# A top-k attention and two MLPs: folded top-k, a one-pass mask, weight splitting on ScalarE

## The chip, the cores and the metric

One core of a Trainium2 chip runs the whole program in one launch. The metric is the device time of the execution in microseconds (us); lower is better. The engines are PE (TensorE), DVE (VectorE), ACT (ScalarE), POOL (GpSimd) and SP, which issues the transfers. Each works through a queue of its own in order; semaphores order the queues against each other.

## The reference

```python
scores = (1 / sqrt(64)) * q @ k.T          # q, k, v: 4 batches, 8 heads, 576 tokens, 64 wide
kth    = 32nd largest score of each row
attn   = softmax(where(scores >= kth, scores, -1e9))
x      = (attn @ v) as 2304 tokens x 512
x      = relu(x @ w_in1) ** 2 @ w_out1     # 512 -> 2048 -> 512
h      = x @ w_in2
out    = (h * clip(h + 3, 0, 6) / 6) @ w_out2
```

The four weight matrices come as 64-bit floats; q, k, v and the result are 32-bit.

## The kernel before

All the work is cut into tasks, each with an engine, a cost in us, a priority and a function that emits its instructions. A planner (`Plan.run`, L71) plays the tasks through in simulated time: whenever an engine is free it takes, of the tasks whose inputs are done and whose buffers are free, the one with the lowest key, and emits it. The key is `offset + slope * position`, with a pair of numbers for each kind of task in the table `PRIO` (L1233). So the order in each engine's queue, SP's loads included, is fixed when the program is built; buffers are counted pools, taken by `alloc` and given back by `free` when named tasks are done.

Weights: each of the four matrices is 16 slabs of 128 x 512. A slab is loaded as 64-bit words, DVE makes 32-bit floats of it in two passes through a PSUM bank of the pool "h" (L372, L375), ACT and POOL add the low bits (L427, L431), PE multiplies blocks with themselves to bound the matrix (L447), and a short chain gives a scale. Then `w_split` writes a slab as two 16-bit halves. `SPE` (L1221) chooses how, by matrix and slab: "e" scales with a 32-bit matmul against a diagonal (L555), ACT evacuates the high half (L558), PE subtracts it (L561), ACT evacuates the low half (L564), in a bank of "h" or in the first accumulator; "a" scales on ACT (L537), copies the high half on ACT (L540) and subtracts on POOL (L543), in SBUF alone. Matmuls use three of the four products of halves.

Attention: for a pair of heads and 128 tokens, PE makes the scores in two PSUM banks (pool "s", one buffer; 64 tokens at the end of a batch are handled for both heads at once), ACT evacuates them with the factor 0.125 to the SBUF tile S (L722, L726, L727), after which "s" is free. For each of 144 head tiles DVE finds the 32 largest by four MAX8 and three MATCH_REPLACE8 over 576 columns (L754, L759, L762), POOL scales the 32nd (L770) and the largest (L766), ACT writes how far each score lies below the 32nd, times a huge factor (Relu, L775), POOL subtracts that from the scores (L778), ACT takes Exp with the row sum (L783) and the high half (L788), POOL the low half (L792, L793), a transposing transfer turns the weights, and PE multiplies them with the values (L811). Eight such tiles make the rows of one MLP unit of 128 tokens; `x_operand` scales and splits them and a transposing transfer (L905) delivers them as the operand `hl`.

MLPs: 18 units, two layers each, 16 blocks of hidden columns a layer (taken in fours as a `group`). A block is 12 matmuls of 128 columns into a bank of "h" (L1046), ACT and DVE apply the nonlinearity (L1053, L1055, L1058, L1061), ACT and POOL split the result (L1068, L1071), and PE accumulates three products of 512 columns (L1078). The two layers accumulate in the two banks of one PSUM tile, `acc_t[:, 0, :]` and `acc_t[:, 1, :]`; the first is read by L959, L283 and L287, which make the operand of the second layer, the second by L1150. The weight stage uses the same two banks, one for the block products and one for scaling.

`prep` loads q, k and v of a head pair and splits them. `SPLIT` (L1219) says for each of the three, and for the first batch and later ones, whether the low half is made by DVE ("d": L283, L287) or by a second ACT pass and POOL ("a": L278, L283, L289).

Of the kernel before, what the change touches and what calls it, by code (L numbers as in the profile page):

```python
# [32 lines left out]
class Plan:  # L33
# [102 lines left out]
def tile_topk_attention_moe_moe2(  # L136
# [83 lines left out]
    acc_t = ps.tile([P, 2, 512], F32, name="acc")  # L220
# [164 lines left out]
    def w_convert(i, n_, pn, par):  # L385
# [55 lines left out]
        def gram():  # L441
            pn["t"] = acc_t[:, 1, :].rearrange("p (c n) -> p c n", c=4)
# [80 lines left out]
    def w_split(i):  # L523
# [6 lines left out]
        for n_, s in enumerate(w_order(i)):  # L530
# [22 lines left out]
            def scaled(x=home(i, n_), box=box, bank=bank):  # L553
                box["t"] = acc_t[:, 0, :] if bank == "acc0" else take("h", "wx")
# [129 lines left out]
    def attend(i, hp):  # L684
# [50 lines left out]
        free("s", ta, tb)  # L735
        masks = [attend_head(i, s, t, hp, hs, ta, tb, box, n_) for n_, (s, t, hs) in enumerate(heads)]
        free("S", tb, *masks)

    def attend_head(i, s, t, hp, hs, ta, tb, sbox, at):
# [7 lines left out]

        def topk(r):

            if r == 0:  # L750
                T["m", s] = take("m")
            m = T["m", s]
            if r == 0:
                nc.vector.max(m[:, 0:8], scores())  # L754
            elif r % 2:
                if r == 1:
                    T["W", s] = take("W")
                c = (r + 1) // 2
                nc.vector.match_replace(out=T["W", s], in_to_replace=m[:, 8 * c - 8:8 * c],  # L759
                                        in_values=scores() if c == 1 else T["W", s], imm_value=-3.0e38)  # L760
# [7 lines left out]
        def lowest():  # L768
            T["kb", s] = take("kb")
            nc.gpsimd.tensor_scalar(T["kb", s], T["m", s][:, TOPK - 1:TOPK], FAR, 1.0, op0=ALU.mult, op1=ALU.mult)  # L770

        def below():

            T["E", s] = take("E")
            nc.scalar.activation(T["E", s], scores(), AF.Relu, bias=T["kb", s], scale=-FAR)  # L775

        def mask():
            nc.gpsimd.tensor_tensor(T["E", s], scores(), T["E", s], op=ALU.subtract)  # L778

        def expo():  # L780
            if t == 0:
                T["sums", i] = take("sums")
            nc.scalar.activation(T["E", s], T["E", s], AF.Exp, bias=T["nb", s], scale=T["scl", b, hp],  # L783
# [31 lines left out]
        prev, ops = tb, []  # L815
        for r in range(7):
            prev = task("DVE", 0.73 if r % 2 else 0.667, ("topk", s + 0.1 * r), lambda r=r: topk(r), deps=[prev],
                        alloc=["m"] if r == 0 else ["W"] if r == 1 else [])
            ops.append(prev)
        free("W", ops[1], ops[6])  # L820
        tn = task("POOL", 0.25, ("bias", s), bias, deps=[ops[0], scl_task[b, hp]], reads=[("scl", b % 2, hp)],
                  alloc=["nb"])
        tk = task("POOL", 0.25, ("lowest", s + 0.7), lowest, deps=[ops[6]], alloc=["kb"])
        free("m", ops[0], tk, tn)
        tr = task("ACT", 0.68, ("below", s), below, deps=[tk, before[1]], alloc=["E"])
        free("kb", tk, tr)
        tm = task("POOL", 1.375, ("mask", s), mask, deps=[tr])
        te = task("ACT", 0.855, ("expo", s), expo, deps=[tn, tm, mask_task.get((i, 0))], reads=[("scl", b % 2, hp)],
# [5 lines left out]
        free("E", tr, tl)  # L834
# [97 lines left out]
    def x2_operand(u):  # L932
# [22 lines left out]
        def square(i):  # L955
# [3 lines left out]
            nc.scalar.activation(box["yh"][r, 0].bitcast(BF16), acc_t[r, 0, :], AF.Square, accum_out=box["ss"][r],  # L959
# [39 lines left out]
        for i in us:  # L999
            lows += split(DM, lambda r=rows(i): acc_t[r, 0, :], [lambda r=rows(i): box["yh"][r, 0]],  # L1000
# [26 lines left out]
    def group(m, u, g):  # L1027
# [45 lines left out]
        def acc(fi, chunks):  # L1073
            f = g * GF + fi
            gl = [box["g"][:, d, fi * n:(fi + 1) * n] for d in range(2)]
            o_ = acc_t[0:n, m, :]
# [59 lines left out]
    def second_layer(u):  # L1136
# [10 lines left out]
        def evac(ch):  # L1147
            rows = min(P, n - ch * P)
            box["o", ch] = take("f", "o")
            nc.scalar.activation(box["o", ch][0:rows], acc_t[0:rows, 1 if n == P else ch, :], AF.Copy,  # L1150
# [52 lines left out]
def first_of(order, b):  # L1203
# [15 lines left out]
SPLIT = {"k": "dd", "q": "aa", "v": "aa"}  # L1219
NPOOL = (4, 4, 4, 4)  # L1220
SPE = ('eeee', 'eeee', 'eeea', 'aaaa')  # L1221
# [12 lines left out]
    "warm": (1282.15, 0.002),  # L1234
    "load0": (777.23, 9.214),
    "load1": (127.78, 60.000),
    "load2": (664.05, 53.961),
    "load3": (-4.07, 7.825),
    "conv0": (45.26, 10.612),
    "bits0": (600.79, 60.000),  # L1240
    "add0": (-237.89, 1.856),
    "gram0": (15.99, 0.354),
    "conv1": (-406.63, 2.819),
    "bits1": (80.52, 6.224),
    "add1": (-235.62, 1.849),
    "gram1": (216.20, 10.049),
    "conv2": (-409.90, 53.003),
    "bits2": (-1760.18, 0.112),
    "add2": (-188.71, 3.740),
    "gram2": (48.70, 10.612),  # L1250
    "conv3": (329.01, 0.042),
    "bits3": (252.65, 10.961),
    "add3": (236.99, 1.853),
    "gram3": (748.44, 8.119),
    "norm": (78.63, 1.217),
    "high0": (62.09, 0.782),
    "low0": (841.85, 0.170),
# [36 lines left out]
    "bias": (41.79, 1.201),
    "lowest": (169.15, 3.401),
    "below": (-48.31, 11.652),
    "mask": (570.67, 0.003),
    "expo": (320.75, 8.491),
    "whigh": (81.64, 0.004),
    "wlow": (-235.69, 0.079),  # L1300
    "wflip": (-279.82, 18.441),
    "av": (-1082.26, 7.037),
    "xinv": (177.41, 30.408),
    "xcopy": (-739.31, 11.224),
    "xflip": (184.59, 0.011),
    "xsquare": (104.09, 6.224),
    "xtotal": (-3717.92, 0.001),
    "xscale": (215.88, 3.937),
    "xevac": (-1218.12, 17.761),
    "xhigh": (168.61, 0.032),  # L1310
    "xlow": (311.27, 0.017),
    "common": (1244.29, 56.386),
    "ysquare": (274.21, 9.900),
    "ytotal": (96.81, 8.609),
    "yflip": (-30.55, 6.067),
    "yscale": (209.78, 27.068),
    "yhigh": (11.75, 18.136),
    "ylow": (364.58, 1.638),
    "whole": (239.48, 8.119),
    "up0": (48.93, 10.612),  # L1320
    "up1": (169.46, 22.110),
    "relu0": (-384.24, 0.640),
    "relu1": (-540.11, 2.304),
    "gsquare": (-3027.59, 0.002),
    "gate": (-335.99, 2.169),
    "ghigh0": (-400.39, 0.035),
    "ghigh1": (370.42, 0.570),
    "glow0": (-1345.79, 8.247),
    "glow1": (110.22, 4.848),
    "acc0": (228.04, 5.723),  # L1330
    "acc1": (192.49, 5.612),
    "oscale": (263.33, 29.118),
    "oevac": (305.73, 1.860),
    "store": (239.89, 2.214),
# [44 lines left out]
```

## Time and profile before

| | us |
|---|---|
| median of 3 runs | 1134.74 (1134.3 to 1134.82) |
| the profiled execution, its time | 1135.86 |
| its span, first to last instruction | 1134.0 |

The profile is of one execution. In its tables "x" is a count of instructions; busy time of an engine is the time in which it ran at least one; a time behind "<-" is idle time of the engine just before an instruction, put down to what ended it. PEclk is the granted share of TensorE's full clock.

### The profile page before, as it was taken

Reading aid. Unit: us, or ns where it says so; the run is one execution under the profiler, and the core shown is the slowest. Engines: PE = TensorE matmul, PEld = TensorE weight load, DVE = VectorE, ACT = ScalarE, POOL = GpSimd, SP = SyncE. Lnnn points to the kernel's source line nnn. Section 1 sums busy time; section 2 is a strip of 40 time slices with the busy share of each in tenths; the row PEclk is TensorE's granted clock in tenths of the full one; section 3 lists DMA queues with packets and bytes.
Section 4 is the critical chain, followed back from the end, with each engine's and each line's share of the span. In section 5 each row is a group of like instructions: output and inputs, shape, how many; then the busy total and the mean of one; then the engine's idle time right before and its main releaser. Section 6 shows DMA issues by size and latency. Waiting matters only on the chain.

```text
span 1134.0 us, 31149 instructions
## 1 busy us (share of the span) xinstructions
PE 1032.9 (91%) x12407; PEld 723.9 (64%) x12407; DVE 939.9 (83%) x2026; ACT 866.8 (76%) x1600; POOL 802.0 (71%) x1041
## 2 busy tenths in 40 slices
PE   3436988889999999999999999999999999999998
PEld 1234446476766776677666767777767767777675
DVE  6999999999778999999989999986799989970010
ACT  6755989799898777888997878878967878773332
POOL 5798767589877677777887878777767867673221
PEclk9985999989999999999999999999999999999999
DMA  8978655224565424343754334434233332431100
GB/s 273 263 227 282 181 120 139 57 52 66 117 121 124 67 53 68 68 62 64 120 114 96 63 73 66 69 72 86 71 63 62 69 72 53 73 72 41 10 20 20
DMA packets 227905, 107.40 MB, mean 95 GB/s; under 512 B 210736, under 2 KB 210736, under 8 KB 227760
## 3 DMA queue, kind: packets, MB, share of 16 engines
q1 hardware_dynamic: 227760, 105.41, 43.0%
q8 instruction: 97, 1.59, 0.6%
q14 instruction: 48, 0.39, 0.1%
HBM read 48.76 MB, written 4.72 MB: 47 GB/s over the span
## 4 chain that ended last, share of the span: by engine, by line
PE 61%; ACT 15%; DVE 13%; issue 4%; POOL 3%; DMA 3%; SPq 0%; ACTq 0%; DVEq 0%; POOLq 0%
PE acc L1078 25%; PE hb L1046 25%; PE av L811 4%; DVE W L759 3%; PE sp L713 3%; DVE m L762 3%; ACT E L775 2%; ACT w L564 1%; DVE m L754 1%; ACT E L783 1%; ACT w L558 1%; DVE cv L372 1%; DVE w L375 1%; ACT wc L788 1%; POOL w L431 1%
## 5 line engine op out<-in xcount | busy, mean ns | idle before, releaser
L1046 PEld LDWEIGHTS <-w 128*128 128x128 f16 x6912 | 424.3, 98 | 105.3 <-issue 5.9
L1078 PE MATMUL acc<-w,ghl 128*128 128x512 f16 x1728 | 460.0, 379 | 12.0 <-DVE xh L287 5.6
L1046 PE MATMUL hb<-hl,w 128*128 128x128 f16 x6912 | 467.2, 220 | 4.0 <-ACT w L564 1.6
L762 DVE MAX8 m<-W 128x8 f32<-128x576 f32 x432 | 314.2, 749 | 1.8
L778 POOL TENSOR_TENSOR E<-S,E 128x576 f32<-128x576 f32 x144 | 203.3, 1414 | 50.6 <-ACT E L775 49.8
L1071 POOL TENSOR_TENSOR ghl<-r,ghl 128x512 f16<-128x512 f32 x144 | 167.3, 1162 | 100.4 <-ACT ghl L1068 88.4
L759 DVE MATCH_REPLACE8 W<-m,W 128x576 f32<-128x576 f32 x288 | 213.2, 742 | 0.0
L1078 PEld LDWEIGHTS <-ghl 128*128 128x128 f16 x1728 | 145.1, 98 | 100.1 <-issue 14.6
L792 POOL TENSOR_TENSOR wc<-E,wc 128x512 f16<-128x512 f32 x144 | 167.8, 1166 | 39.5 <-ACT wc L788 37.6
L775 ACT ACTIVATE E<-S,scalars 128x576 f32<-128x576 f32 x144 | 111.5, 775 | 35.6 <-POOL scalars L770 33.4
L783 ACT ACTIVATE E<-E,scalars 128x576 f32<-128x576 f32 x144 | 125.1, 869 | 17.0 <-POOL E L778 16.6
L754 DVE MAX8 m<-S 128x8 f32<-128x576 f32 x144 | 107.1, 748 | 22.6 <-ACT S L722 16.4
L1061 DVE SCALAR_TENSOR_TENSOR r<-r,hb 128x512 f32<-128x512 f32 x72 | 48.8, 678 | 78.2 <-ACT r L1055 77.3
L759 DVE MATCH_REPLACE8 W<-m,S 128x576 f32<-128x576 f32 x144 | 106.7, 742 | 0.0
L1068 ACT ACTIVATE ghl<-r 128x512 f16<-128x512 f32 x144 | 90.4, 628 | 19.9 <-DVE r L1061 17.0
L788 ACT ACTIVATE wc<-E 128x576 f16<-128x576 f32 x144 | 98.1, 681 | 0.7
L811 PEld LDWEIGHTS <-wT 128*128 128x128 f16 (+1 forms) x2240 | 82.4, 102 | 19.3 <-issue 6.5
L1055 ACT ACTIVATE r<-hb,bias,scalars 128x512 f32<-128x512 f32 x72 | 55.7, 774 | 47.3 <-PE hb L1046 43.6
L811 PE MATMUL av<-vv,wT 128*128 128x64 f16 (+1 forms) x2240 | 91.0, 196 | 0.7 <-DMA wT<-wc 0.7
L431 POOL TENSOR_TENSOR w<-w,stg 128x512 int32<-128x512 int32 x57 | 72.6, 1285 | 25.1 <-DVE w L375 9.2
L1053 ACT ACTIVATE r<-hb 128x512 f32<-128x512 f32 x72 | 43.1, 598 | 57.2 <-PE hb L1046 56.7
L726 ACT ACTIVATE S<-sp 128x1024 f32<-128x1024 f32 x64 | 65.3, 1020 | 14.5 <-POOL E L778 14.2
(113 smaller groups left out, 1208.2 us busy)
## 6 DMA issues: line engine op xcount, KB each, us to landing
w<-in_moe_w_in_dram SPq DMA_DIRECT2D x32, 512.0 KB, 6.4
w<-in_moe_w_out_dram SPq DMA_DIRECT2D x29, 512.0 KB, 4.2
stg<-in_k_dram SPq DMA_DIRECT2D x16, 320.0 KB, 3.2
stg<-in_v_dram SPq DMA_DIRECT2D x16, 320.0 KB, 3.8
stg<-in_q_dram SPq DMA_DIRECT2D x16, 288.0 KB, 3.9
out_dram<-o SPq DMA_DIRECT2D x16, 256.0 KB, 2.1
wT<-wc SPq DMA_TRANSPOSE x144, 3.3
stg<-in_moe_w_out_dram SPq DMA_DIRECT2D x6, 256.0 KB, 3.5
```

The costliest lines, as they stand in the source:

```text
L754: nc.vector.max(m[:, 0:8], scores())
L759: nc.vector.match_replace(out=T["W", s], in_to_replace=m[:, 8 * c - 8:8 * c], in_values=scores() if c == 1 else T["W", s], imm_value=-3.0e38)
L762: nc.vector.max(m[:, 4 * r:4 * r + 8], T["W", s])
L775: nc.scalar.activation(T["E", s], scores(), AF.Relu, bias=T["kb", s], scale=-FAR)
L778: nc.gpsimd.tensor_tensor(T["E", s], scores(), T["E", s], op=ALU.subtract)
L783: nc.scalar.activation(T["E", s], T["E", s], AF.Exp, bias=T["nb", s], scale=T["scl", b, hp], accum_out=T["sums", i][:, t:t + 1])
L788: nc.scalar.activation(T["wc", s][:, 0:S], T["E", s], AF.Copy)
L792: nc.gpsimd.tensor_tensor(wc[:, S + TAIL:], e[:, 0:S - TAIL], wc[:, 0:S - TAIL], op=ALU.subtract)
L811: nc.tensor.matmul(out_[cols, t * D:(t + 1) * D], wT[0:kr, a, cols], vv[0:kr, vb, hh, c, :], start=n_ == 0, stop=n_ == len(prods) - 1)
L1046: nc.tensor.matmul(box["h"][:, fi * n:(fi + 1) * n], wt[2 * m][:, kk * 4 + f // 4, a, f % 4 * P:(f % 4 + 1) * P], hl[:, c, kk, 0:n], start ...
L1071: nc.gpsimd.tensor_tensor(flat(box["g"][:, 1]), flat(box["r"]), flat(box["g"][:, 0]), op=ALU.subtract)
L1078: nc.tensor.matmul(o_, gl[d], wt[2 * m + 1][:, f, a, :], start=f == 0 and (a, d) == (0, 0), stop=f == KF - 1 and (a, d) == PRODS[-1])
```

## The change

Top-k first folds the two halves of a tile: the larger of each pair of columns goes into the first half of W, the smaller into the second. The first two rounds of eight search the 288 larger ones only, the last two all 576 (only a row with more than 16 of its 32 largest in pairs of one another would need more). A fold reads one half from PSUM, so "s" is freed when the folds of both heads are done too. The mask becomes one Prelu on ACT, whose scale, bias and negative slope make a score at or above the 32nd its scaled distance to it and any other a huge negative number; Exp loses its scale, and POOL's subtraction is gone. `SPE` and `SPLIT` move work from PE and DVE to ACT and POOL. The accumulators become two tiles. `PRIO` gets a third number per kind of task and all new values.

```diff
-        offset, slope = PRIO[key[0]]
-        t = Task(eng, cost, offset + slope * key[1], fn, tuple(alloc), lat or LAT[eng])
+        offset, slope, bend = PRIO[key[0]]
+        t = Task(eng, cost, offset + slope * key[1] + bend * max(0.0, key[1] - 20.0), fn, tuple(alloc), lat or LAT[eng])
...
-    acc_t = ps.tile([P, 2, 512], F32, name="acc")
+    acc_t = [ps.tile([P, 512], F32, name=f"acc{m}") for m in range(2)]
...
-        free("s", ta, tb)
-        masks = [attend_head(i, s, t, hp, hs, ta, tb, box, n_) for n_, (s, t, hs) in enumerate(heads)]
-        free("S", tb, *masks)
+        done = [attend_head(i, s, t, hp, hs, ta, tb, box, n_) for n_, (s, t, hs) in enumerate(heads)]
+        free("s", ta, tb, *[x[1] for x in done])
+        free("S", tb, *[x[0] for x in done])
...
+        def fold(op):
+            if op == ALU.max:
+                T["W", s] = take("W")
+            lo = HALF if op == ALU.min else 0
+            nc.vector.scalar_tensor_tensor(T["W", s][:, lo:lo + HALF], sbox["sp"][:, 0 if tail else at, 0:HALF], 0.125,
+                                           scores()[:, HALF:S], op0=ALU.mult, op1=op)
...
+            m, c = T["m", s], r // 2
+            w = lists()[:, 0:S if r > 3 else HALF]
+            if r % 2:
+                nc.vector.match_replace(out=w, in_to_replace=m[:, 8 * c:8 * c + 8], in_values=w, imm_value=-3.0e38)
             else:
-                nc.vector.max(m[:, 4 * r:4 * r + 8], T["W", s])
+                nc.vector.max(m[:, 8 * c:8 * c + 8], w)
+
+        def lowest():
+            T["kb", s] = take("kb")
+            nc.gpsimd.tensor_scalar(T["kb", s], T["m", s][:, TOPK - 1:TOPK], T["scl", b, hp], -1.0, op0=ALU.mult,
+                                    op1=ALU.mult)
 
         def bias():
             T["nb", s] = take("nb")
-            nc.gpsimd.tensor_scalar(T["nb", s], T["m", s][:, 0:1], T["scl", b, hp], -1.0, op0=ALU.mult, op1=ALU.mult)
...
+            nc.gpsimd.tensor_scalar(T["nb", s], T["m", s][:, TOPK - 1:TOPK], T["m", s][:, 0:1], T["scl", b, hp],
+                                    op0=ALU.subtract, op1=ALU.mult)
...
-            nc.scalar.activation(T["E", s], scores(), AF.Relu, bias=T["kb", s], scale=-FAR)
-
-        def mask():
-            nc.gpsimd.tensor_tensor(T["E", s], scores(), T["E", s], op=ALU.subtract)
+            nc.scalar.activation(T["E", s], scores(), AF.Prelu, bias=T["kb", s], scale=T["scl", b, hp], alpha=FAR)
...
-            nc.scalar.activation(T["E", s], T["E", s], AF.Exp, bias=T["nb", s], scale=T["scl", b, hp],
+            nc.scalar.activation(T["E", s], T["E", s], AF.Exp, bias=T["nb", s],
...
+        prev = f1 = task("DVE", 0.39, ("fold", s), lambda: fold(ALU.max), deps=[tb], alloc=["W"])
+        prev = f2 = task("DVE", 0.39, ("fold", s), lambda: fold(ALU.min), deps=[f1])
...
-SPLIT = {"k": "dd", "q": "aa", "v": "aa"}
+SPLIT = {"k": "aa", "q": "aa", "v": "aa"}
...
-SPE = ('eeee', 'eeee', 'eeea', 'aaaa')
+SPE = ('eeee', 'aaaa', 'aaaa', 'aaaa')
```

## Rows read from the trace of the kernel before

**Rows 1.** The page, busy time and share of the span by engine:
```profile
PE 1032.9 (91%) x12407; PEld 723.9 (64%) x12407; DVE 939.9 (83%) x2026; ACT 866.8 (76%) x1600; POOL 802.0 (71%) x1041
```

**Rows 2.** Busy time by stage (stretch, length, each engine, PEclk, DMA share, GB/s):
```profile
108.00:270.00 162.00, 143.74 (x1341) 87.17 (x1341) 153.57 (x335) 144.40 (x273) 115.08 (x147) 0.96 0.47 114
270.00:1026.00 756.00, 743.25 (x9561) 533.54 (x9560) 677.32 (x1480) 617.59 (x1147) 576.03 (x773) 1.00 0.42 78
```

**Rows 3.** The same, the matmuls of L1046 alone:
```profile
108.00:270.00 162.00, 31.86 (x456) 29.45 (x456) 0.96 0.47 114
```

**Rows 4.** Timeline of PE at 714 us (start us, us, engine, line):
```profile
714.01 0.83 PE L1046 MATMUL hb<-hl,w 128*128 128x128 f16 x12
...
715.33 0.83 PE L1046 MATMUL hb<-hl,w 128*128 128x128 f16 x12
```

**Rows 5.** Timeline of SP, transfers that deliver MLP operands:
```profile
139.64 1.23 SPq L905 DMA_TRANSPOSE hl<-xh  x1
...
215.82 1.35 SPq L905 DMA_TRANSPOSE hl<-xh  x1
...
270.44 1.23 SPq L905 DMA_TRANSPOSE hl<-xh  x1
```

**Rows 6.** Timeline of DVE at 503 us:
```profile
503.20 0.74 DVE L762 MAX8 m<-W 128x8 f32<-128x576 f32 x1
503.87 0.07 DVE L759 MATCH_VALUE_LOAD W<-m,S 128x8 f32 x1
...
504.58 0.08 DVE L759 MATCH_VALUE_LOAD W<-m,W 128x8 f32 x1
```

**Rows 7.** Groups by line and shape (busy us, mean ns | idle before):
```profile
L778 POOL TENSOR_TENSOR E<-S,E 128x576 f32<-128x576 f32 x144 | 203.3, 1414 | 50.6 <-ACT E L775 49.8
...
L783 ACT ACTIVATE E<-E,scalars 128x576 f32<-128x576 f32 x144 | 125.1, 869 | 17.0 <-POOL E L778 16.6
L775 ACT ACTIVATE E<-S,scalars 128x576 f32<-128x576 f32 x144 | 111.5, 775 | 35.6 <-POOL scalars L770 33.4 <-POOL wc L793 2.1
...
L1061 DVE SCALAR_TENSOR_TENSOR r<-r,hb 128x512 f32<-128x512 f32 x72 | 48.8, 678 | 78.2 <-ACT r L1055 77.3 <-POOL wc L793 0.8
...
L372 DVE TENSOR_SCALAR cv<-w 128x512 int32<-128x512 int32 x61 | 41.4, 684 | 9.3 <-DMA w<-in_moe_w_in_dram 6.5 <-ACT w L564 1.7 <-DMA w<-in_moe_w_out_dram 0.9
...
L564 ACT ACTIVATE w<-wx 128x512 f16<-128x512 f32 x34 | 20.5, 613 | 0.7 <-PE wx L561 0.7
...
L287 DVE SCALAR_TENSOR_TENSOR kT<-stg,hsc,kT 128x640 f16<-128x640 f32 x16 | 17.9, 1119 | 4.8 <-ACT kT L283 4.8
...
L537 ACT ACTIVATE stg<-w,scalars 128x512 f32<-128x512 f32 x20 | 14.7, 759 | 0.0
...
L540 ACT ACTIVATE w<-stg 128x512 f16<-128x512 f32 x20 | 13.2, 669 | 0.0
...
L372 DVE TENSOR_SCALAR cv<-stg 128x256 int32<-128x256 int32 x6 | 2.5, 420 | 0.1
...
L627 ACT ACT_TABLE_LOAD x1 | 1.3, 1283 | 0.7 <-PEq L1348 0.7
```

**Rows 8.** Busy time by stage, the scaling matmuls of L555 alone:
```profile
108.00:270.00 162.00, 46.97 (x88) 13.93 (x87) 0.96 0.47 114
```

**Rows 9.** Timeline of all engines at 1080 us:
```profile
1080.21 0.19 ACT L959 ACTIVATION_READ_ACCUMULATOR xh<-acc 128x1 f32 x1
1080.45 0.81 PE L1078 MATMUL acc<-w,ghl 128*128 128x512 f16 x3
```

**Rows 10.** Waits of PE, 324 to 1020 us (total us, times, longest):
```profile
PE acc L1078 <- DVE xh L287: 3.8, 8, 1.6
PE acc L1078 <- ACT xh L283: 1.9, 6, 0.6
PE acc L1078 <- ACT xh L959: 1.5, 5, 0.6
...
PE sp L713 <- ACT S L726: 0.2, 1, 0.2
```

More of the change, by code (lines that the diff above doesn't have):

```diff
@@ L553, in scaled @@
             def scaled(x=home(i, n_), box=box, bank=bank):
-                box["t"] = acc_t[:, 0, :] if bank == "acc0" else take("h", "wx")
+                box["t"] = acc_t[0] if bank == "acc0" else take("h", "wx")
                 nc.tensor.matmul(box["t"], diag, x, start=True, stop=True)
@@ L1316 @@
[L1316 to L1331, printed above, removed]
@@ L1332 @@
-    "oscale": (263.33, 29.118),
-    "oevac": (305.73, 1.860),
-    "store": (239.89, 2.214),
+    "fold": (110.2430, 22.51530, 30.86830),
+    "warm": (48.5705, 55.32380, -4.56282),
+    "load0": (508.6360, 8.67045, 11.68850),
+    "load1": (-654.7650, 0.07494, -0.07394),
+    "load2": (1397.9200, 60.00000, -13.72010),
+    "load3": (118.3160, 10.41650, -0.80200),
+    "conv0": (19.2278, 5.07288, 1.90793),
+    "bits0": (570.9830, 7.20295, 1.90239),
+    "add0": (-924.5550, 1.07846, 31.09350),
@@ new lines @@
+    "gram0": (-25.2149, 32.93760, 12.67230),
+    "conv1": (118.9040, 16.60550, -0.09529),
+    "bits1": (1371.7600, 0.01058, 0.64252),
+    "add1": (-4152.4500, 0.03495, -0.03102),
+    "gram1": (-336.4380, 60.00000, 7.04352),
+    "conv2": (-6.0664, 1.26428, 4.69135),
+    "bits2": (-99.3023, 36.87820, 12.78040),
+    "add2": (-4119.3900, 0.03469, 11.31450),
+    "gram2": (547.9510, 0.57617, -0.86162),
+    "conv3": (-93.0884, 28.25930, -3.00368),
+    "bits3": (-651.8930, 0.00499, -0.00258),
@@ new lines @@
+    "add3": (-4172.9300, 0.03495, -0.03395),
+    "gram3": (24.6435, 14.22760, 0.36460),
+    "norm": (-3482.5200, 0.00864, -0.01529),
+    "high0": (-256.2210, 0.29526, -0.29426),
+    "low0": (542.0990, 13.32040, -0.79653),
+    "scaled0": (12.8753, 2.10067, 6.19248),
+    "rest0": (181.5110, 1.55960, -0.46063),
+    "high1": (166.3500, 60.00000, 2.25513),
+    "low1": (231.1430, 14.76260, 8.93547),
+    "scaled1": (-53.3252, 7.26384, -4.42694),
+    "rest1": (-164.7600, 1.66391, 3.93547),
+    "high2": (574.5610, 21.87670, 3.56963),
@@ new lines @@
+    "low2": (874.4770, 60.00000, -9.96385),
+    "scaled2": (-179.2780, 52.44380, -16.56670),
+    "rest2": (1095.4100, 28.28930, -11.13780),
+    "high3": (1514.7000, 0.28361, 0.25372),
+    "low3": (645.4610, 28.81770, -1.52273),
+    "scaled3": (-845.8960, 1.28399, 22.20350),
+    "rest3": (-97.7912, 8.56906, 5.91166),
+    "qsquare": (-848.5390, 0.06317, 0.15313),
+    "kqtotal": (670.5070, 3.56410, 0.86650),
+    "kqscale": (910.5360, 15.15100, 0.07630),
+    "total": (-4839.0600, 0.00120, 6.21917),
@@ new lines @@
+    "scale": (-343.3880, 0.07275, -0.07766),
+    "ksquare": (-624.1050, 0.00780, 18.82520),
+    "vsquare": (142.4190, 0.38887, 10.36680),
+    "vtotal": (708.9630, 0.35309, 18.83140),
+    "vscale": (-178.0370, 2.00116, -0.73305),
+    "kload": (-30.7745, 60.00000, -0.41157),
+    "vload": (385.7370, 6.10508, -6.10408),
+    "qload": (123.6830, 16.50910, 0.70091),
+    "qhigh": (-323.0800, 0.21422, -0.32405),
+    "qlow": (-330.8830, 7.62098, -7.61998),
+    "khigh": (-4070.0400, 0.04425, -0.08551),
@@ new lines @@
+    "klow": (157.2820, 23.33330, 3.76432),
+    "vhigh": (429.9100, 27.68430, -2.24825),
+    "vlow": (2038.9800, 0.46545, 3.31071),
+    "qscales": (462.3060, 48.97140, -9.13526),
+    "qk": (132.8680, 0.68496, 8.53916),
+    "evac": (66.1182, 24.55520, 0.81225),
+    "topk": (654.6280, 31.03460, -1.46628),
+    "bias": (-1057.7200, 0.67536, 1.85076),
+    "lowest": (-358.3980, 0.54492, 0.16230),
+    "below": (758.4220, 0.80896, 17.26030),
+    "expo": (66.7798, 4.02526, 26.82630),
+    "whigh": (-453.5540, 0.19395, 22.90810),
@@ new lines @@
+    "wlow": (-387.6150, 49.29990, 9.97620),
+    "wflip": (552.8500, 1.53137, 11.48750),
+    "av": (-1145.5400, 0.04952, 4.06439),
+    "xinv": (-882.9890, 0.03386, 15.23920),
+    "xcopy": (-14.9756, 1.93658, 12.77230),
+    "xflip": (8.4723, 1.99725, 2.17467),
+    "xsquare": (547.7130, 0.24135, 2.23321),
+    "xtotal": (-270.7630, 3.14983, 5.45422),
+    "xscale": (-3225.9100, 0.02498, -0.01779),
+    "xevac": (-3521.7100, 25.36230, 1.79440),
+    "xhigh": (-458.3500, 0.00254, 6.48265),
+    "xlow": (-501.6510, 14.76440, 0.01290),
@@ new lines @@
+    "common": (445.1980, 4.51653, 0.16734),
+    "ysquare": (422.7410, 17.05150, 11.72350),
+    "ytotal": (-410.2410, 3.03014, 2.31279),
+    "yflip": (-175.6640, 1.54102, 14.09590),
+    "yscale": (114.6990, 23.33330, 5.00635),
+    "yhigh": (-348.1600, 0.05563, 4.16612),
+    "ylow": (-57.4212, 22.93520, 1.98205),
+    "whole": (-3638.4000, 0.18876, 1.49656),
+    "up0": (334.0050, 4.88609, 2.39978),
+    "up1": (168.0120, 53.43270, 13.15750),
+    "relu0": (-1374.1500, 0.01335, -0.01235),
+    "relu1": (-2164.4200, 0.22905, 2.33372),
@@ L1335 @@
+    "gsquare": (737.6780, 0.00654, 6.94544),
+    "gate": (0.8930, 32.93760, -5.09384),
+    "ghigh0": (-279.9930, 0.06336, -2.72340),
+    "ghigh1": (-298.5840, 28.55680, 2.89029),
+    "glow0": (1381.3400, 9.21088, 13.41230),
+    "glow1": (-183.6340, 60.00000, 1.60895),
+    "acc0": (595.4470, 3.98126, 0.07970),
+    "acc1": (391.7790, 6.10508, 4.00145),
+    "oscale": (-710.9470, 9.39983, 11.76290),
+    "oevac": (-216.8060, 0.51395, 6.92382),
+    "store": (620.4360, 1.53289, 5.54577),
 }
```

132 lines of the change are left out of this document (20 added, 112 removed).

## The prediction

> **What bounds the kernel now.** I read the busy line of the page first. The reader is to see that TensorE is busy 91% of the span and VectorE 83%, ScalarE 76%, GpSimd 71% [rows 1]: no engine but TensorE is near its span, but a mean over stages decides nothing. So I cut the span into stages [rows 2]. From 270 to 1026 us TensorE is busy 743.3 of 756 us, VectorE 677. From 108 to 270 us it is the other way: VectorE is at 153.6 of 162, ScalarE at 144.4, and TensorE's 143.7 hold a lot that isn't MLP: only 456 matmuls of L1046 [rows 3], 38 blocks of 12, of the 576 blocks that the kernel has (18 units, two layers, 16 blocks).
>
> The timeline of a full stretch shows what a saturated TensorE is: from the start of one block of 12 to the next, 1.32 us, the three accumulations of an earlier block between them [rows 4]. So 576 blocks are 760 us, and the 538 left at 270 us are 710 of the 864 us that remain; score and value matmuls fill most of the rest. That stage can't be shortened except by having more blocks behind it when it begins, or by taking out the few us of idle time.
>
> What kept the blocks from being done before 270 us? The transposes that deliver a unit's operand answer it [rows 5]. The first is issued at 139.6 us, the second at 215.8, the third at 270.4. A unit is eight head tiles, and each layer of it is 16 × 1.32 = 21 us of TensorE. The second operand, not TensorE, is late: 76 us after the first, the third only 55 after that. Before 270 us the kernel waits for attention and for converted weights, after it for TensorE. These are two bounds, one after the other, and the change is priced in each.
>
> **The change, part by part.**
>
> *Top-k.* A tile's chain on VectorE is four maxima and three replacements of 576 columns. By their starts a maximum takes 0.67 us (503.20 to 503.87) and a replacement with its value load 0.71 (503.87 to 504.58) [rows 6]: 4 × 0.67 + 3 × 0.71 = 4.81 us. Four of the seven go to 288 columns. No row shows a maximum of 288, but an operation at 512 and 256 columns took 684 and 420 ns [rows 7], 1.03 ns a column, so 288 fewer are 0.30 us: 0.37 and 0.41. Two folds are added. The nearest row is the gate, also two tensors with one in PSUM: 678 ns at 512 columns [rows 7], 0.45 at 288, and 0.37 if it overlaps its neighbour as the maxima do. I take 0.40, between the two: 0.80 + 2 × 0.37 + 2 × 0.41 + 2 × 0.67 + 0.71 = 4.41. A tile saves 0.40 us (0.31 to 0.46), 144 tiles 58 us of VectorE. [...]
>
> *Mask.* GpSimd's subtraction, 144 × 1.414 us = 203 us [rows 7], goes. On ScalarE Relu with one pointer (775 ns) becomes Prelu with two, and Exp loses one (869 ns with two) [rows 7]: if Prelu costs what the others do, the two passes swap prices, nothing. Bounds: nothing, to 0.094 us a tile, 14 us in all, if Exp keeps its time. The chain from the maxima to Exp loses one hop of 1.41 us and its two waits, which is latency. If Prelu needed another function table, see the rivals.
>
> *Weights.* Diff and code say that 28 of 64 slabs move from TensorE to ScalarE and GpSimd (before 44 by TensorE, after 16). Scaling a slab is two matmuls; all 88 of them, 47.0 us, lie between 108 and 270 us [rows 8]: 1.07 us a slab, 30 us for 28. ScalarE pays 759 + 669 ns in place of two evacuations of 613 [rows 7], 0.20 more, 5.7 us over 28. GpSimd pays about 1.26 us a slab (the 576-column row scaled to 512), 35 us, out of the 203 it was given. TensorE isn't the bound there, so this gives no time by itself. It frees both PSUM "h" banks that scaling, bit conversion and MLP blocks share, and makes room there for blocks that come earlier.
>
> *Keys.* The low half of k leaves VectorE (1.12 us, 16 times [rows 7]) for GpSimd (about 1.6 by the 576 row), and ScalarE gets a second pass (about 0.7): 18 us off VectorE in all, 4.5 in the first batch's four, 12 us more for ScalarE.
>
> *Accumulators.* At 1080.21 to 1080.40 us ScalarE reads the accumulator of layer one, and TensorE's accumulation starts at 1080.45 [rows 9]. The layer-one bank isn't free for a next unit before VectorE too has read it, so this was layer two, in the other bank: the two banks of one tile wait for each other. Between 324 and 1020 us the waits of accumulations for these three readers are 1.5, 1.9 and 3.8 us [rows 10]. The first two can't be real by this argument; the third may be. Two tiles give back 3.4 to 7.2 us of saturated TensorE; I take 5.
>
> *Score banks.* They are now freed when both heads' folds are done, not when the evacuation is. Scores of the next pair wait on TensorE behind them, and behind those the MLP. Today that queue lost 0.2 us to the evacuation [rows 10]. After a pair's second fold VectorE still has the first head's seven operations, 4.41 − 0.80 = 3.6 us; the planner's 0.93 for scores and 1.15 for evacuation fit in it with 1.5 us to spare. I cost this at nothing; the top-k queue is the cover, and without it each of 80 score tasks (64 pairs, 16 tails) could stall TensorE.
>
> *New priorities* reorder every queue, the loads of SP too. No row prices this; I bound it with the stage.
>
> **The sum.** *Start.* 24 tiles stand before the third operand: 24 × 0.40 + 4.5 = 14 us less VectorE work ahead of it. That is the lower end, where order and latency give nothing. The upper end is a second operand that also comes 55 us after the first, not 76: 21.6 more, 36. The work taken from PSUM, GpSimd's masks and TensorE all lies in this stage, so I take 30, nearer the top. *Saturated stage.* 5 us from the accumulators; of the 12.8 us idle in 756 the rest I leave. Removing VectorE's other work there gives nothing, since TensorE covers it. 1134.0 − 30 − 5 = 1099.0 span, plus the 1.9 us that lie around it, 1100.9; the profiled execution is 1.1 above the median of the runs, so 1099.7. I say 1099.
>
> **Rivals.**
>
> *The start stays where it is.* ScalarE is at 89% between 108 and 270 us [rows 2], and the change gives it 5.7 us more of weights. If it, not VectorE, delivers the second operand, only the accumulators' 3 to 7 us are won: 1128 to 1131 beside a median of 1134.7, and with the 5.7 us ahead of the operands 1133 to 1137.
>
> *TensorE waits for folds* (the other side). One late fold holds scores, and scores hold the MLP in TensorE's queue. 80 score tasks share a gain of 35 us, so 0.44 us each is break-even; 0.65 would be 1099 + 52 = 1151. For it: the bank is single, and a stall in a full engine is not given back. Against it: 1.5 us to spare, and VectorE 8% lighter.
>
> *Prelu switches tables.* The one table load took 1283 ns [rows 7], and today's functions share it. If Prelu lay elsewhere, 144 tiles would take up to 288 loads, 370 us: ScalarE at 867 + 18 + 370 = 1255, which is the time at least. Against the 214 us that ScalarE has to spare at 1099, some 167 loads decide. [...]
>
> *Order gives more.* If the first operand too comes earlier by 25 us, as its weights do, 1074.
>
> **How the numbers follow.** The forecast, start earlier by 14 to 36 us, has 0.67: 1091 to 1117. More from order 0.12, about 1074. Start unmoved 0.10: half of it faster, 0.04 the same, 0.01 slower. Fold waits 0.08, tables 0.03. Within 0.2% (2.3 us) is about what a measurement of this kernel can't tell from no change. Faster is 0.67 + 0.12 + 0.05 = 0.84, same 0.04, slower 0.12. The range leaves out the slow rivals and the far end of order: 1070 to 1124.
>
> **What would show it.** Right: maxima of 288 columns near 0.37 by their starts; GpSimd near 670 us; second and third operands 14 to 36 us earlier; TensorE as dense from there on; no accumulation waiting for layer one's readers while the other bank is used. Wrong: more than one table load; score matmuls waiting for folds; operands at 216 and 270 us as before, with ScalarE full ahead of them; a TensorE that falls under 97% in the long stage because attention is late in the new order.

## The result, and the profile after

The changed kernel takes 1098.51 us (median of four runs, 1098.3 to 1099.84) beside 1134.52 for the kernel before on the same chip (four runs, 1132.14 to 1134.82): 0.969 of its time, interval 0.9673 to 0.9706, or 36 us less. The profiled execution took 1098.36 us, its span 1096.6.

The page after, its span and the busy time of each engine:

```profile
span 1096.6 us, 31039 instructions
PE 1002.6 (91%) x12323; PEld 715.7 (65%) x12323; DVE 856.1 (78%) x2298; ACT 878.5 (80%) x1616; POOL 676.0 (62%) x941
```

Against [rows 1], VectorE lost 84 us, GpSimd 126, TensorE 30, and ScalarE gained 12. None of these differences is the 36 us. As before the place to look is the stages; all engines first, then the matmuls of the MLP's first step alone (L1046 before, L1052 now):

```profile
108.00:270.00 162.00, 126.04 (x1429) 89.34 (x1428) 154.97 (x402) 156.05 (x292) 137.23 (x176) 0.86 0.51 121
270.00:1026.00 756.00, 754.87 (x9748) 544.94 (x9747) 599.27 (x1672) 622.75 (x1149) 443.62 (x658) 1.00 0.42 78
...
108.00:270.00 162.00, 44.12 (x624) 40.71 (x624) 0.86 0.51 121
270.00:1026.00 756.00, 378.85 (x5748) 345.25 (x5748) 1.00 0.42 78
```

The counts are a ledger of the gain. Before 270 us there are 624 matmuls in place of 456 [rows 3], 14 more blocks of 12, which at 1.32 us a block [rows 4] are 18.5 us. From 270 to 1026 us there are 5748 in place of 5592, 13 more blocks, 17.2 us, and TensorE is busy 754.87 us of that stretch in place of 743.25 [rows 2]. At 1026 us the new kernel is thus 27 blocks ahead: 35.6 of the 37.4 us by which the span is shorter. About one half was won ahead of 270 us, the other half as density behind it. (The ledger counts a block by its first step. Of the accumulations, 125 in place of 100 ran before 270 us, 8 blocks more and not 14, so the first half is somewhat smaller than 18.5 us.)

All 14 blocks come between 216 and 270 us. At 216 us both kernels have done 192 of these matmuls, one layer of one unit; in the 54 us behind it they do 264 and 432. For the kernel before, all engines in these 54 us and in the second half of them, its matmuls of L1046, its scaling (L555) and the subtraction that belongs to it (L561); last, L1052 of the changed kernel:

```profile
216.00:270.00 54.00, 47.73 (x501) 31.66 (x499) 51.33 (x117) 50.80 (x99) 42.86 (x59) 0.91 0.35 59
243.00:270.00 27.00, 26.89 (x284) 16.80 (x282) 24.47 (x54) 26.81 (x53) 23.70 (x32) 1.00 0.29 46
...
216.00:270.00 54.00, 19.01 (x264) 18.03 (x264) 0.91 0.35 59
...
216.00:270.00 54.00, 8.46 (x16) 2.64 (x16) 0.91 0.35 59
216.00:270.00 54.00, 3.71 (x9) 0.81 (x9) 0.91 0.35 59
...
216.00:270.00 54.00, 26.73 (x432) 24.83 (x432) 1.00 0.35 63
```

TensorE was busy 47.7 of the 54 us before, and 12.2 us of that were scaling, of which the changed kernel has none here.

The transposes that deliver the operands of the first four units:

```profile
138.12 1.23 SPq L911 DMA_TRANSPOSE hl<-xh  x1
209.69 1.23 SPq L911 DMA_TRANSPOSE hl<-xh  x1
257.26 1.23 SPq L911 DMA_TRANSPOSE hl<-xh  x1
302.47 1.34 SPq L911 DMA_TRANSPOSE hl<-xh  x1
```

The first three come 1.5, 6.1 and 13.2 us earlier than in [rows 5]. The fourth was at 319.8 before, so 17.3. The 6.1 us by which the second comes earlier are an estimated 5 of the 14 blocks at 1.32 us each. The trace suggests the 12.2 us of TensorE as the source of the others; no run shows it by itself.

All that TensorE waited for from 270 to 1026 us (total, times, longest), which answers [rows 10]:

```profile
PE acc L1084 <- DVE xh L287: 0.5, 1, 0.5
PE sp L713 <- DVE W L752: 0.2, 1, 0.2
```

The changed operations, by shape (busy time, mean ns of one, idle time before them), answering [rows 7]:

```profile
L767 DVE MAX8 m<-W 128x8 f32<-128x576 f32 x288 | 212.7, 750 | 1.2
L765 DVE MATCH_REPLACE8 W<-m,W 128x288 f32<-128x288 f32 x288 | 126.8, 443 | 0.0
L767 DVE MAX8 m<-W 128x8 f32<-128x288 f32 x288 | 124.7, 449 | 0.6
L782 ACT ACTIVATE E<-S,scalars 128x576 f32<-128x576 f32 x144 | 124.2, 863 | 45.6 <-POOL scalars L771 27.6 <-POOL wc L797 17.2
L787 ACT ACTIVATE E<-E,scalars 128x576 f32<-128x576 f32 x144 | 110.9, 770 | 1.7
...
L543 POOL TENSOR_TENSOR w<-stg,w 128x512 f16<-128x512 f32 x48 | 54.9, 1164 | 3.6 <-ACT w L540 3.6
L537 ACT ACTIVATE stg<-w,scalars 128x512 f32<-128x512 f32 x48 | 34.0, 722 | 1.1 <-DVE scalars L272 0.8 <-POOL w L543 0.2
...
L627 ACT ACT_TABLE_LOAD x1 | 1.3, 1283 | 0.7 <-PEq L1354 0.7
```

There is still one load of a function table. Prelu (L782) takes 863 ns and Exp (L787) 770, where Exp took 869 and Relu 775 [rows 7]: the swap.

The timeline of VectorE in the long stage, for the price by starts:

```profile
499.21 0.81 DVE L767 MAX8 m<-W 128x8 f32<-128x288 f32 x2
499.93 0.07 DVE L765 MATCH_VALUE_LOAD W<-m,W 128x8 f32 x1
499.99 0.44 DVE L765 MATCH_REPLACE8 W<-m,W 128x288 f32<-128x288 f32 x1
500.35 0.08 DVE L765 MATCH_VALUE_LOAD W<-m,W 128x8 f32 x1
...
508.73 1.55 DVE L752 SCALAR_TENSOR_TENSOR W<-sp,S 128x288 f32<-128x288 f32 x4 [1.62 <-ACT S L727]
```

Two maxima of 288 columns take 0.72 us from start to start, 0.36 each; a replacement with its value load 0.42; four folds 1.55, with a mean duration of 0.447 about 0.37 each by their starts.

What holds the start now is seen in slices of 27 us (columns as in the stages):

```profile
135.00:162.00 27.00, 19.08 (x223) 16.31 (x224) 24.93 (x55) 26.86 (x50) 27.00 (x30) 0.69 0.88 226
162.00:189.00 27.00, 20.70 (x196) 13.21 (x195) 26.24 (x68) 26.28 (x47) 27.00 (x32) 0.82 0.57 143
...
243.00:270.00 27.00, 25.24 (x338) 18.56 (x338) 26.81 (x76) 27.00 (x53) 22.81 (x34) 1.00 0.32 61
```

ScalarE and GpSimd fill them to 26.3 us and more between 135 and 189, and VectorE nearly so. In the whole stage GpSimd is busy 137 us in place of 115 [rows 2], although its masks are gone.

### The profile page after: what moved, and what is told of

Same layout as the page of the kernel before. It is cut to its first block, busy times and chain, and to the rows that moved or that the text cites. A ratio compares the mean times of both kernels' runs of the same rounds, so it can differ in the third digit from the quotient of the medians.

```text
span 1096.6 us, 31039 instructions
## 1 busy us (share of the span) xinstructions
PE 1002.6 (91%) x12323; PEld 715.7 (65%) x12323; DVE 856.1 (78%) x2298; ACT 878.5 (80%) x1616; POOL 676.0 (62%) x941
## 4 chain that ended last, share of the span: by engine, by line
PE 71%; DVE 7%; ACT 2%; issue 1%; POOL 1%; POOLq 0%; ACTq 0%; DVEq 0%
PE hb L1052 31%; PE acc L1084 30%; PE av L815 5%; PE sp L713 3%; DVE m L767 2%; DVE W L765 2%; PE spare L716 1%; PE sp L707 1%; DVE W L752 1%; DVE r L1067 0%; DVE xh L287 0%; ACT r L1061 0%; ACT E L782 0%; ACT ghl L1074 0%; ACT xh L283 0%
## 5 line engine op out<-in xcount | busy, mean ns | idle before, releaser
L1052 PEld LDWEIGHTS <-w 128*128 128x128 f16 x6912 | 419.4, 99 | 77.4 <-issue 0.3
L1052 PE MATMUL hb<-hl,w 128*128 128x128 f16 x6912 | 459.7, 220 | 0.2
L1084 PE MATMUL acc<-w,ghl 128*128 128x512 f16 x1728 | 445.1, 381 | 8.0 <-ACT ghl L1074 4.1
L767 DVE MAX8 m<-W 128x8 f32<-128x576 f32 (+1 forms) x576 | 329.7, 599 | 1.8
L765 DVE MATCH_REPLACE8 W<-m,W 128x288 f32<-128x288 f32 (+1 forms) x432 | 233.0, 543 | 0.0
L782 ACT ACTIVATE E<-S,scalars 128x576 f32<-128x576 f32 x144 | 124.2, 863 | 45.6 <-POOL scalars L771 27.6
L752 DVE SCALAR_TENSOR_TENSOR W<-sp,S 128x288 f32<-128x288 f32 x288 | 122.6, 447 | 33.7 <-ACT S L722 17.4
L787 ACT ACTIVATE E<-E,scalars 128x576 f32<-128x576 f32 x144 | 110.9, 770 | 1.7
L776 POOL TENSOR_SCALAR scalars<-m,scalars 128x1 f32<-128x1 f32 x144 | 52.4, 364 | 71.8 <-DVE m L767 64.3
L447 PE MATMUL acc<-w 128*128 128x128 bf16 x256 | 30.6, 255 | 38.9 <-POOL w L431 31.3
```

The lines of the kernel that those rows point to most:

```text
L752: nc.vector.scalar_tensor_tensor(T["W", s][:, lo:lo + HALF], sbox["sp"][:, 0 if tail else at, 0:HALF], 0.125, scores()[:, HALF:S], op0=ALU ...
L765: nc.vector.match_replace(out=w, in_to_replace=m[:, 8 * c:8 * c + 8], in_values=w, imm_value=-3.0e38)
L767: nc.vector.max(m[:, 8 * c:8 * c + 8], w)
L782: nc.scalar.activation(T["E", s], scores(), AF.Prelu, bias=T["kb", s], scale=T["scl", b, hp], alpha=FAR)
L1052: nc.tensor.matmul(box["h"][:, fi * n:(fi + 1) * n], wt[2 * m][:, kk * 4 + f // 4, a, f % 4 * P:(f % 4 + 1) * P], hl[:, c, kk, 0:n], start ...
L1084: nc.tensor.matmul(o_, gl[d], wt[2 * m + 1][:, f, a, :], start=f == 0 and (a, d) == (0, 0), stop=f == KF - 1 and (a, d) == PRODS[-1])
```

## The experiments

Of two things the profile can't decide how much each was worth: the accumulators, and what came early at the start. Most of the kernels below change one thing. "Order kept" means that the sequence of every engine's queue is that of the kernel it was made from; "numbers searched anew" means that the table of priorities was made for that kernel. Differences between medians of different chips carry about 1 us: the kernel before ran at 1134.1 to 1135.3 beside them.

**The accumulators, from both ends.** First the changed kernel with both in one tile again, order kept:

```diff
-    acc_t = [ps.tile([P, 512], F32, name=f"acc{m}") for m in range(2)]
+    acc_2 = ps.tile([P, 2, 512], F32, name="acc"); acc_t = [acc_2[:, m, :] for m in range(2)]
```

> The changed kernel, but both accumulators in one tile again; every queue keeps its order. The prediction's term: the waits of accumulations for the layer-one readers come back, 3 to 7 us (1102 to 1106). Rival: the changed kernel's stage from 270 to 1026 us has 1.1 us of idle TensorE where there were 12.8, and some 17 us fewer for the same blocks; if the tiles made all of that, 1110 to 1116. Second rival: the planner's new order made it, and the tiles give nothing: 1097 to 1100.

Measured: 1113.43 us (1112.87 to 1113.67), 0.9819 of before [0.9794, 0.9844]. That is 15 us lost, not 3 to 7. The matmuls of L1052 by stage, then TensorE's longest waits for accumulator readers from 270 to 1026 us:

```profile
108.00:270.00 162.00, 42.97 (x594) 39.79 (x595) 0.86 0.51 121
270.00:1026.00 756.00, 371.72 (x5638) 338.25 (x5636) 1.00 0.41 78
...
PE acc L1084 <- DVE xh L287: 3.2, 7, 0.9
...
PE acc L1084 <- ACT xh L283: 1.0, 2, 0.6
...
PE acc L1084 <- ACT xh L965: 0.2, 1, 0.2
```

By the ledger 9.2 blocks (12.1 us) are missing in the long stage, and 2.5 (3.3 us) ahead of it, where the second and third operands come 2.5 and 2.8 us later. So in this order the two tiles help in the start too; the weight stage uses the same two banks.

Then the other end: the kernel before with two tiles, order kept, the six uses of `acc_t` written as `acc_t[0]` and `acc_t[1]`.

> The kernel before, but with two accumulator tiles; every queue keeps its order. The prediction's term: 3 to 7 us less (1127 to 1131 where it measures 1134.5), with the waits of accumulations for the layer-one readers gone. Rival, the tiles made the whole denser stage: 12 to 17 us less (1117 to 1123). Second rival, they give nothing: within 2 us.

Measured: 1118.82 us (1117.87 to 1120.36), 0.9867 [0.9836, 0.9899]. 15 us again, with the operands where they were (215.4 and 269.9 us). Its stages:

```profile
270.00:1026.00 756.00, 751.24 (x9724) 541.43 (x9723) 677.48 (x1480) 621.59 (x1158) 579.55 (x776) 1.00 0.43 79
...
270.00:1026.00 756.00, 383.38 (x5700) 347.78 (x5699) 1.00 0.43 79
```

The second line is L1046 alone: 5700 matmuls in place of 5592, 9 blocks or 11.9 us in this stretch, while the named waits that left it were 7.2 us [rows 10]. So the rows named the waits rightly and too small. Part of the rest is an overlap, which the row between the two of [rows 4] shows:

```profile
714.68 0.81 PE L1078 MATMUL acc<-w,ghl 128*128 128x512 f16 x3
```

The block's row began at 714.01 and lasts 0.83 us, and the next instruction starts 0.67 after it began, so a wait begins 0.16 us before its idle time shows. There are 19 named waits here and four behind 1026 us, which took 2.5 us by name; an estimated 0.16 us for each of the 23 is 3.7 us. That makes 13.4 of the 15.3 us. What remains, some two us, I can't name.

**The widths of top-k, early and late.** In the changed kernel 24 of the 144 tiles search all 576 columns in every round, 28.5 us more VectorE work, order kept: in the first kernel (the upper of the two new lines) the first 24 tiles, in the second 24 tiles in the middle.

```diff
-            w = lists()[:, 0:S if r > 3 else HALF]
+            w = lists()[:, 0:S if r > 3 or s < 24 else HALF]
+            w = lists()[:, 0:S if r > 3 or 60 <= s < 84 else HALF]
```

> The changed kernel with its order, but the first 24 head tiles search and replace all 576 columns in all seven operations: four operations of each are 0.30 us longer, 28.5 us of VectorE ahead of the third operand, 19 ahead of the second. If VectorE's top-k gates the start, as the prediction has it: second and third operand 15 to 28 us later, and the time up by about the delay of the third operand and what follows, 15 to 28 us (1113 to 1127). Rival: ScalarE and GpSimd, full from 135 to 270 us, gate it, and VectorE has room: under 8 us.

Measured: 1114.99 us (1114.78 to 1116.44), 0.9836 [0.9811, 0.9862]. 16.5 us lost, and the third operand is 16.6 us later (273.89 us): in the start the time follows the operands.

> The same 28.5 us of VectorE, but in 24 head tiles of the middle (60 to 83), when TensorE is the bound. Prediction: covered by TensorE, 0 to 3 us (1098 to 1102). Rival, VectorE still sets the pace in the middle: 15 to 28 us (1113 to 1127).

Measured: 1123.79 us (1122.58 to 1124.68), 0.991 [0.9884, 0.9936]. Of 28.5 us put on an engine with slack, 25.3 came out at the end, where I had expected hardly any. The stage by parts, and the longest waits:

```profile
270.00:466.00 196.00, 194.73 (x2528) 138.92 (x2526) 164.56 (x453) 168.32 (x313) 118.48 (x175) 1.00 0.43 91
466.00:645.00 179.00, 160.59 (x2006) 115.61 (x2004) 152.61 (x360) 140.50 (x262) 100.03 (x148) 0.98 0.42 79
645.00:1026.00 381.00, 380.33 (x4915) 274.22 (x4913) 305.38 (x849) 304.22 (x559) 218.35 (x332) 1.00 0.40 69
...
PE sp L713 <- DVE W L752: 9.6, 7, 2.5
```

TensorE is idle for 18 us in the stretch of the wide tiles. Its longest wait is for folds, which hold the pool "s" of one buffer, and the MLP stands behind those scores in its queue. This is the rival in which TensorE waits for folds, made real by a late VectorE. VectorE is not full even there. Is it VectorE, or the queue's order, made for short tiles? The same kernel with the planner told of the longer tiles, and the numbers searched anew:

> The changed kernel with the same 24 middle tiles widened as in the fixed-order run (28.5 us more VectorE, which cost 25 us there), but the planner is told the longer costs and has priority numbers searched anew for them. If TensorE really covers VectorE in the middle, as the prediction has it, and only the fixed order made the 25 us: 1098 to 1106. Rival, attention and MLP are both critical there and no order helps: 1115 to 1125.

Measured: 1098.74 us (1097.48 to 1101.15), 0.9685 [0.9667, 0.9703]: nothing lost.

```profile
270.00:1026.00 756.00, 753.97 (x9735) 543.96 (x9733) 624.07 (x1667) 620.63 (x1146) 441.59 (x656) 1.00 0.41 77
```

VectorE carries 25 us more in this stage than in the changed kernel, and TensorE is as dense. The new numbers didn't make the time up elsewhere: L1052 has 620 matmuls before 270 us (624 in the changed kernel) and 5768 in this stage (5748). The work was covered; the fixed order had not been made to cover it.

**The mask and the width of top-k, in the order of before.** On the kernel before with two tiles, order kept. The first leaves out the subtraction on GpSimd:

```diff
-            nc.gpsimd.tensor_tensor(T["E", s], scores(), T["E", s], op=ALU.subtract)
+            pass
...
-FAR = 2.0 ** 96
+FAR = 1.0
```

> The kernel before with two accumulator tiles (1118.8 us), order kept, without GpSimd's mask subtraction (it leaves that step of the computation out): 203 us of GpSimd and one hop in each head tile's chain go, nothing else. Prediction: the mask counts in the start alone, a few us of the 20 that still lie between this and the changed kernel: 1111 to 1117. Rival, the hop and GpSimd's load set the pace of attention: 1100 to 1109. Second rival, covered everywhere: within 2 us of 1118.8.

The second narrows one replacement, so that a tile's chain on VectorE loses what the folded one loses:

```diff
+                n_ = 192 if r == 3 else S
-                nc.vector.match_replace(out=T["W", s], in_to_replace=m[:, 8 * c - 8:8 * c],
-                                        in_values=scores() if c == 1 else T["W", s], imm_value=-3.0e38)
+                nc.vector.match_replace(out=T["W", s][:, 0:n_], in_to_replace=m[:, 8 * c - 8:8 * c],
+                                        in_values=scores() if c == 1 else T["W", s][:, 0:n_], imm_value=-3.0e38)
```

> The kernel before with two accumulator tiles (1118.8 us), order kept; the second of the three replacements works on 192 of 576 columns (it leaves part of that step out), 0.40 us less VectorE in each head tile, 57 us in all, which is what the folds save. Prediction: only the 24 tiles of the start count, 6 to 14 us (1105 to 1113). Rival, VectorE also sets the pace in the middle, as the 25 us that the widened middle tiles cost say: 18 us or more, to about 1100 or below. Second rival, the fixed order gives nothing back when an engine gets faster: within 4 us of 1118.8.

The third does both:

> The kernel before with two accumulator tiles (1118.8 us), order kept, without the mask subtraction and with the shorter replacement together (alone they gave 6.0 and 6.9 us; both leave those steps out). If they shorten the same chain one after the other: 1104 to 1108. If they cover each other, since another engine follows close behind: 1109 to 1113. If the two engines had to get free together, more than the sum: below 1103.

| kernel | us (lowest to highest) | ratio [interval] | less than two tiles alone |
|---|---|---|---|
| no subtraction | 1112.85 (1112.44 to 1114.55) | 0.981 [0.9785, 0.9836] | 6.0 |
| shorter top-k | 1111.94 (1110.44 to 1114.31) | 0.980 [0.9775, 0.9826] | 6.9 |
| both | 1105.6 (1105.36 to 1105.81) | 0.9743 [0.9727, 0.9759] | 13.2 |

The two add up. Removing 203 us of GpSimd, with the hop that goes along, gives 6, and 57 us of VectorE gives 7. The matmuls of the MLP's first step by stage, in the kernel with both:

```profile
108.00:270.00 162.00, 35.62 (x536) 32.81 (x537) 0.98 0.47 108
270.00:1026.00 756.00, 386.78 (x5748) 350.82 (x5745) 1.00 0.42 78
```

With two tiles alone there are 457 and 5700. So 6.6 blocks (8.7 us) are won before 270 us and 4 (5.3 us) in the stage from 270 to 1026 us, where TensorE's named waits fall from 4.1 us to 0.7. The second and third operands of the three kernels come 4.4 and 5.6, 2.8 and 3.8, 8.1 and 9.5 us earlier than with two tiles alone. In the shorter top-k 24 tiles are 9.6 us of VectorE ahead of the third operand, and the operand gained 3.8 of it.

**The folds alone, with an order of their own.** The kernel before with two tiles and the folded top-k, its mask, weights and keys left as they were, numbers searched anew:

> The kernel before with two accumulator tiles and the folded top-k, without the one-pass mask and with the weights and keys split as before; priority numbers searched anew. If the top-k is what the start waits for: 1102 to 1112. Rival, without the other parts' room on GpSimd and in PSUM a shorter top-k buys nothing: 1114 to 1122.

Measured: 1114.87 us (1110.61 to 1116.09), 0.9817 [0.9794, 0.9841], 4 us less than two tiles alone. The shorter top-k had given 7. The kernel misses the range for a start that waits for the top-k (1102 to 1112) and lies at the lower end of the rival's; and since its interval overlaps that of two tiles alone, even the 4 us are not certain.

**The order.** The changed kernel with the priorities of before, and a value for the folds that puts them in the place of the first maximum:

```diff
-    "fold": (110.2430, 22.51530, 30.86830),
+    "fold": (732.08, 24.128, 0.0),
...
```

> The changed kernel with all its parts, but planned with the priority numbers of before (bend 0, the folds with the numbers of the top-k). If the parts carry the gain and the order little: 1098 to 1110. Rival: the numbers are made for exact costs, and parts without new numbers give no more than the accumulators' 15 us, or lose: 1115 to 1145.

Measured: 1130.75 us (ten runs, 1128.98 to 1133.25), 0.9968 [0.9956, 0.9981]. All the parts together, the accumulators among them, give 3 us (the kernel before took 1134.14 on this chip) with numbers made for others. The queues are not those of before: the planner played the new tasks with the old numbers.

```profile
270.00:1026.00 756.00, 736.04 (x9467) 528.76 (x9466) 608.97 (x1690) 616.73 (x1141) 439.60 (x661) 1.00 0.42 77
```

Here the first operand is issued at 123.7 us, 16 earlier than before, but the second at 230.0, 14 later, and TensorE falls to 97.4% in the long stage. The early first operand didn't make up for that.

**The fold's source.** A fold reads one half from PSUM, which ties the score banks to it. Reading both halves from SBUF frees the banks at the evacuation:

```diff
-            nc.vector.scalar_tensor_tensor(T["W", s][:, lo:lo + HALF], sbox["sp"][:, 0 if tail else at, 0:HALF], 0.125,
+            nc.vector.scalar_tensor_tensor(T["W", s][:, lo:lo + HALF], scores()[:, 0:HALF], 1.0,
```

> The changed kernel, order kept, but the folds read both halves from the evacuated scores in SBUF, so the score banks wait for the evacuation alone. Prediction: TensorE waits for folds only 2 us in all, so 0 to 2 us less (1096.5 to 1099). Rival: with two SBUF inputs VectorE and GpSimd disturb each other, 5 us or more slower, with longer folds or GpSimd subtractions in the rows.

Measured: 1155.62 us (1155.46 to 1156.41), 1.0185 [1.0163, 1.0206], 57 us lost. The fold's line with its durations (least, median, most):

```profile
L752 DVE SCALAR_TENSOR_TENSOR W<-S x288: 429/449/6552, 16.1 to 1024.9; 128x288 f32<-128x288 f32 x144
...
L752 DVE SCALAR_TENSOR_TENSOR W<-S 128x288 f32<-128x288 f32 x288 | 194.7, 696 | 28.5 <-ACT S L722 16.9 <-ACT S L727 11.4
```

The median is that of the fold from PSUM, the mean is 696 ns in place of 447: 72 us more of VectorE. Which folds are long is seen by laying VectorE's timeline beside GpSimd's (start, length):

```profile
572.14 1.56 DVE L752 SCALAR_TENSOR_TENSOR W<-S 128x288 f32<-128x288 f32 x4
580.63 0.97 DVE L752 SCALAR_TENSOR_TENSOR W<-S 128x288 f32<-128x288 f32 x1
582.26 1.40 DVE L752 SCALAR_TENSOR_TENSOR W<-S 128x288 f32<-128x288 f32 x1
...
570.60 1.16 POOL L1077 TENSOR_TENSOR ghl<-r,ghl 128x512 f16<-128x512 f32 x1
573.38 1.34 POOL L796 TENSOR_TENSOR wc<-E,wc 128x512 f16<-128x512 f32 x1 [1.62 <-issue]
579.88 1.41 POOL L289 TENSOR_TENSOR vv<-stg,vv 128x640 f16<-128x640 f32 x1
582.06 1.28 POOL L289 TENSOR_TENSOR qT<-stg,qT 128x576 f16<-128x576 f32 x1
```

The four folds at 572.14 run while GpSimd idles, but for their last 0.3 us, and take 1.56 us. The one at 580.63 ends 0.31 us behind a GpSimd pass that ends at 581.29, the one at 582.26 ends 0.32 behind one that ends at 583.34. Of the 66 folds of over 0.55 us that stand by themselves in the timeline, 62 end 0.30 to 0.33 us behind the end of a GpSimd pass over two tensors. They waited for GpSimd to finish.

## Why the prediction was right, and where only its sum was

**Two bounds, one after the other**: right in the main. The ledger splits the gain at 270 us into 18.5 and 17.2 us, and the wide early tiles cost the time by which the operands are late. But the border lies earlier than 270 us: from 243 to 270 us TensorE was already busy 26.89 of 27 us.

**Top-k**: right in its prices, 0.36, 0.42 and 0.37 us where it had 0.37, 0.41 and 0.40, so a tile saves some 0.46 us, its upper end. The folded search is exact for every row of scores, also for one with its 32 largest in 16 pairs: a value taken in the first two rounds has at most 30 larger ones, 15 maxima and their 15 partners, and the last two rounds find the 16 largest of what is left.

**Mask**: right. Prelu and Exp swap prices, and GpSimd ended at 676 us, near the 670. The hop that the prediction called latency and GpSimd's 203 us are together worth 6 us in the order of before; the runs don't part them.

**Weights and keys**: prices right in kind (ScalarE's two passes 722 and 629 ns, GpSimd's 1164, all a little under the terms; the keys on GpSimd 1404, where it had about 1.6 us). "So this gives no time by itself" was tried by no kernel here, since moving these parts moves the order of every queue. The trace speaks against it: between 216 and 270 us, where the lead arises, the change takes 12.2 us of scaling off a TensorE that was busy 47.7 of 54 us. The term read TensorE's slack from a mean over 162 us. The moved parts fill ScalarE and GpSimd between 135 and 189 us.

**Accumulators**: the mechanism was right, the size was not. "I take 5" was 15, measured from both ends, and in the changed kernel 3 of them lie in the start, where the prediction had none. The step that failed is reading the gain off named waits.

**Score banks at nothing**: right. TensorE waited 0.2 us for a fold in the long stage and 1.0 between 108 and 270 us. The cover is thin, though: with top-k 1.2 us a tile longer in 24 tiles and the same order, these waits grow to 9.6 us, in a kernel that loses 25.

**Removing VectorE's other work in the long stage gives nothing**: right in one direction only: in an order made for it, 25 us more of VectorE there cost nothing. But less work gave something. Of the 17.2 us won there the two tiles are 12.1, by the kernel with one tile, and 5.1 remain, a term that the sum didn't have. In the order of before, the shorter top-k with the mask left out won 5.3 us there.

**New priorities, not priced**: the whole of the difference between 1130.75 and 1098.51 hangs on them. What they would give the kernel before alone wasn't tried; the folds with numbers of their own came to 1114.87 us, so new numbers don't bring the gain without the other parts.

**Start**: this is the term that was too large. "So I take 30, nearer the top" was about 20 (36 less the 15), and by the ledger only some 15 of these lie ahead of 270 us (18.5 less the tiles' 3.3). The second and third operands came 6 and 13 us earlier, not 14 to 36. Its lower end, VectorE's 14 us ahead of the third operand, was taken as passed on whole, but the shorter top-k passed on 3.8 of 9.6, and the wide early tiles 16.6 of 28.5. VectorE was never alone there: of the 162 us ScalarE is busy 144 and GpSimd 115 [rows 2], and the change fills them more, to 156 and 137. Of the 20 us, 6 and 7 are shown for mask and top-k in the old order, two thirds of it ahead of 270 us. The other 7 stay with weights, keys and the new order, and the runs don't part them.

So 1099 was met by 30 + 5 where the runs gave about 20 + 15: two terms missed by the same 10 us, in opposite directions. That the sum came out to the microsecond is luck.

**Rivals.** The start did move, though half as far. TensorE hardly waited for folds. Prelu loaded no table: the one load of 1283 ns is there as before. What a switch would have cost was an estimate, and no run shows it. Order didn't bring the first operand 25 us earlier. The old numbers brought it 16 earlier, but the second 14 later, so what an early first operand is worth is not shown.

## What to carry to other kernels

Count the work done at a fixed time, here the matmul blocks before 270 and 1026 us: such a ledger splits a gain by place, where busy shares and named waits (7 us named, 12 found in the same stretch) don't. In queues whose order is fixed, slack on an engine may cover new work only if the order is made anew for it: here the same 28.5 us cost 25 in the given order and nothing in one of their own. A freed engine is worth what its neighbours leave: 203 us off GpSimd and 57 off VectorE gave 13 together, where three engines share the chain from the scores to the operand. And cut a stage finer before calling an engine free in it: TensorE's 144 of 162 us hid a slice with 26.89 of 27.

## What the runs showed of the hardware that I had not expected

The size of the collision between VectorE and GpSimd: reading both inputs from SBUF in place of one from PSUM turned a mean of 447 ns into 696, at an unchanged median (448 and 449 ns), and cost the kernel 57 us. By the timeline long folds end just behind the GpSimd pass that they met, those at 580.63 and 582.26 us 0.31 and 0.32 us behind it. GpSimd is longer there too: its one-column operation L776 has a mean of 476 ns in that kernel (its longest 1593), and 364 in the changed one (its longest 380).

The granted clock fell in the start: a mean of 0.86 from 108 to 270 us in place of 0.96 [rows 2], 0.69 from 135 to 162 (0.50 in each microsecond from 135 to 147 and 1.00 in each from 148 to 158), in a stretch in which TensorE had less to do (126 us busy in place of 144). It is back at 1.00 from 216 us on, where the kernel before had 0.91 to 270 us; a part of the 14 blocks may be due to that. Whether the low clock cost any of the start wasn't tried. No loss shows in the four runs: their clocks over the whole span are 0.961 to 0.977, and the slowest, 1099.84 us, is the one at 0.977.
